# One pool for all eight PSUM banks, a planner that knows the port lock and instruction fetch, and three raw buffers in place of six

## The chip, the cores and the metric

The kernel runs on one core of a Trainium2 chip. The metric is the time of one execution in microseconds (us) of the device; lower is better. Each kernel was run several times beside runs of the kernel before on the same chip. A run is called fast when it lies within 1.5% of the fastest run of the same kernel there, and slow otherwise. Ratios are the mean of one kernel's fast runs over the mean of the other's fast runs of the same rounds, so they are not quite the ratio of the medians that are quoted too. The span of a profile is about 2 us shorter than the time.

## The reference, cut to what matters

```python
# attention half: q, k, v of shape (8, 8, 576, 64)
q_p, k_p = phi(q), phi(k)            # relu, times cos and sin of the position, 128 features
kv  = einsum('bhsf,bhsd->bhfd', k_p, v);  z = sum(k_p, axis=2)
x   = (q_p @ kv) / (q_p @ z + 1e-6)  # (8, 576, 512) once the heads are put together
# mixing half
wq, wk = x @ w_q, x @ w_k            # 512 -> 64
mixed  = (wq @ wk.T / 8) @ x
out    = relu(mixed) @ w_out         # 512 -> 512, the output projection
```

Inputs and output are float32. 29.6 MB are read and 9.4 MB written.

## The kernel before: the parts that matter

The work is cut into 16 steps of the attention half (a step `H` is four heads of one batch entry: 576 KB each of q, k and v), eight batch entries of the mixing half, and 36 row tiles of the output projection (`wo`, four matmuls of 128x512 each). POOL turns the raw inputs into bfloat16 (`rq`, `rk`, `rv`), DVE multiplies k by cos and sin (`mk`, tile `kp`), PE does the rest, ACT and DVE empty PSUM. SP issues all loads and nearly all stores.

The order in which every engine gets its instructions is not written by hand. A planner runs at build time: it keeps a clock for each engine, gives every operation a cost and its data dependences, and always takes the candidate with the smallest start time, less a small bonus for priority. The chip then waits only for data and buffers, but each engine works through its queue in that order.

```python
op(("load", nm, H), {"DMA": 1.51}, [ago(i >= 3, "r" + "qkv"[i % 3], i // 3)])  # i counts from -nraw
...
op(("qT", H), {"PE": .27}, [ago(H, "rq", H), ago(H, "kve", H - 1)], pa, "row")
...
op(("wo", p, rt), {"PE": .86}, need, pw, "full", 1)
...
after = dict(PE=.13, ACT=.07, DVE=.07, POOL=.1, DMA=.4)   # us until a result may be used
...
key = s - .1 * o["prio"]                                  # PE: start, less a tenth of the priority
...
inp = ctx.enter_context(tc.tile_pool(name="inp", bufs=PLAN["nraw"]))   # raw inputs, 6 buffers
...
K0, N0, M0, M1, M2, M3 = 0, 2, 4, 5, 6, 7                 # PSUM banks: qT and kv; numerators; the rest
```

Of the kernel before, what the change touches and what calls it, by code (L numbers as in the profile page):

```python
# [23 lines left out]
PLAN = dict(mk=1.5, pa=7.057, pc=7.377, pm=6.4, pw=5.394, pb=0.0, flex=.249, poe=3.15, pme=3.3,  # L24
            pmk=.82, wo_at=4, nraw=6, nout=10)


def plan_order(NB, par=None):

    par = {**PLAN, **(par or {})}  # L30
    B = NB // 2
    ops = {}

    def op(name, cost, deps, prio=0.0, mode=None, banks=0, frees=None):
        ops[name] = dict(cost=cost, deps=[d for d in dict.fromkeys(deps) if d],
                         prio=prio, mode=mode, banks=banks, frees=frees)
# [5 lines left out]
    for H in range(NB):  # L42
# [11 lines left out]
        op(("qT", H), {"PE": .27}, [ago(H, "rq", H), ago(H, "kve", H - 1)], pa, "row")  # L54
        for r in range(2):
            op(("qe", H, r), {"DVE": .72}, [("qT", H), ago(H > 1, "num", H - 2, r)], 3)
        op(("kv", H), {"PE": .58}, [ago(H, "mk", H), ago(H, "rv", H), ("qe", H, 0),
                                    ("qe", H, 1)], pa, "row")
        op(("kve", H), {"ACT": 1.05, "DVE": .8}, [("kv", H)], 3)
        for r in range(2):  # L60
            prev = ("norm", H, 0) if r else ago(H, "norm", H - 1, 1)
            op(("num", H, r), {"PE": .33}, [("kve", H), ("qe", H, r), prev], pa, "row")
            op(("norm", H, r), {"DVE": 1.08}, [("num", H, r), ago(b > 2, "kx", b - 3)], 2)
# [4 lines left out]
    for b in range(B):  # L68
        old = [("mx", b - 2, j) for j in range(4)] if b > 1 else []
        op(("wqk", b), {"PE": 1.0},  # L70
           [("xe", H, j) for H in (2 * b, 2 * b + 1) for j in range(2)] + [("cw", 0)],
           pc, "full", 2)
        op(("we", b), {"ACT": .66, "DVE": .78}, [("wqk", b)] + old, 4,
# [4 lines left out]
        op(("kx", b), {"PE": .55}, [("wke", b)], pc, "full", 1)  # L78
        op(("kxe", b), {"ACT": .38, "DVE": .44}, [("kx", b)] + old, 4,
# [6 lines left out]
    for p in range(B // 2):  # L86
        for rt in range(9):
# [4 lines left out]
            if p == 0:  # L92
                need += [("cw", c) for c in range(1, 5)]
            op(("wo", p, rt), {"PE": .86}, need, pw, "full", 1)
            i = 9 * p + rt - par["nout"]
            op(("oe", p, rt), {"ACT": .60, "DVE": .71},
               [("wo", p, rt), ago(i >= 0, "st", i // 9, i % 9)], par["poe"],
# [17 lines left out]
    mode, bank, own, done, order, nload = "full", [0.0] * 4, {}, {}, [], 0  # L115
# [6 lines left out]
    while ready:  # L122
        best = None
        for n, t in ready.items():
# [3 lines left out]
            for e, c in o["cost"].items():  # L128
                s, mine = max(free[e], t), None
                if e == "PE":  # L130
                    s = max(free[e] + (.1 if o["mode"] != mode else 0), t)
                    if o["banks"] == 2:
                        u = min((0, 2), key=lambda i: max(bank[i], bank[i + 1]))
                        s, mine = max(s, bank[u], bank[u + 1]), (u, u + 1)
                    elif o["banks"] == 1:
                        s = max(s, min(bank))
                        u = max((i for i in range(4) if bank[i] <= s),
                                key=lambda i: bank[i ^ 1])
                        mine = (u,)
                    key = s - .1 * o["prio"]  # L140
# [11 lines left out]
        if e == "PE":  # L152
            gap = s - free[e]
            if gap > .9 and bank[3] <= free[e]:
                order.append((("warm", int(gap / .45)), "PE", None))
            mode = o["mode"]
        free[e] = s + c
# [23 lines left out]
def kernel(  # L181
# [15 lines left out]
    P = 128  # L197
# [32 lines left out]
    K0, N0, M0, M1, M2, M3 = 0, 2, 4, 5, 6, 7  # L230
# [25 lines left out]
    def warm_up(n):  # L256
        for _ in range(n):
            nc.tensor.matmul(bank(M3)[:, 0, :], warm[:, 0:P], warm,  # L258
                             start=True, stop=True)

    warm_up(13)
# [118 lines left out]
    def qT_mm(H):  # L380
        for c in range(C9):
            for r in range(2):
                nc.tensor.transpose(  # L383
                    bank_h(K0 + r)[:, 0, c * D:(c + 1) * D],
# [3 lines left out]
    def qT_evac(H, r):  # L388
        nc.vector.tensor_mul(  # L389
            qpt_bufs[H % 2][:, r, :, D:SLOTS * D],  # L390
            bank_h(K0 + r)[:, 0:1, 0:HC].to_broadcast([P, 2, HC]), cst)

    def kv_mm(H):
        for c in range(C9):
            for i in range(2):
                for r in range(2):
                    nc.tensor.matmul(  # L397
                        bank(K0 + r)[:, 0, i * (D + 1):(i + 1) * (D + 1)],
# [4 lines left out]
    def kv_evac(H, eng):  # L403
        kv_sb = small.tile([P, 2, KW], BF16, name="kv_sb")
        kv_sh = small.tile([P, 2, D + 1], BF16, name="kv_sh")
        src = bank(K0, 2)
# [5 lines left out]
    def num_mm(H, r):  # L412
# [240 lines left out]
```

## Time and profile before

| what | before |
|---|---|
| time, median of the four runs beside the changed kernel | 133.81 us (133.13 to 136.04) |
| span of the profile | 130.8 us |
| mean clock granted to PE | 0.974 |
| PE busy | 105.8 us |
| data moved | 39.40 MB at 301 GB/s, 375 to 378 while loads last |

POOL's waits for loads in the kernel before (engine, tile and line, what it waited for: us in total, times, longest):

```profile
POOL rq_buf L348 <- DMA raw<-in_q_dram: 7.9, 6, 2.9
POOL v_buf L373 <- DMA raw<-in_v_dram: 6.6, 10, 0.8
POOL rk L348 <- DMA raw<-in_k_dram: 2.7, 5, 1.9
```

POOL stands 17.2 us for loads, spread over the whole loading time.

### The profile page before, as it was taken

Reading aid. Unit: us, or ns where it says so; the run is one execution under the profiler, and the core shown is the slowest. Engines: PE = TensorE matmul, PEld = TensorE weight load, DVE = VectorE, ACT = ScalarE, POOL = GpSimd, SP = SyncE. Lnnn points to the kernel's source line nnn. Section 1 sums busy time; section 2 is a strip of 40 time slices with the busy share of each in tenths; the row PEclk is TensorE's granted clock in tenths of the full one; section 3 lists DMA queues with packets and bytes.
Section 4 is the critical chain, followed back from the end, with each engine's and each line's share of the span. In section 5 each row is a group of like instructions: output and inputs, shape, how many; then the busy total and the mean of one; then the engine's idle time right before and its main releaser. Section 6 shows DMA issues by size and latency. Waiting matters only on the chain.

```text
span 130.8 us, 5363 instructions
## 1 busy us (share of the span) xinstructions
PE 105.8 (81%) x2279; PEld 61.8 (47%) x2279; DVE 93.8 (72%) x153; ACT 78.5 (60%) x154; POOL 76.8 (59%) x121
## 2 busy tenths in 40 slices
PE   5947685885699989986999699889947999899930
PEld 2325253563546546643756366556624664443300
DVE  1065979689994999959999987989659876346200
ACT  6950063658756796639557595787637865655440
POOL 7728988896779999975697876885371000000000
PEclk9999999999959999999999999999999999999995
DMA  3999999999999999999999999999974034837973
GB/s 88 369 383 394 345 310 403 394 388 390 389 393 388 374 391 396 401 378 376 316 393 413 368 359 378 383 373 295 382 214 87 5 80 89 177 75 167 211 226 110
DMA packets 21239, 39.40 MB, mean 301 GB/s; under 512 B 3040, under 2 KB 4576, under 8 KB 21216
## 3 DMA queue, kind: packets, MB, share of 16 engines
q1 hardware_dynamic: 20544, 38.08, 85.0%
q10 hardware_dynamic: 672, 0.98, 2.5%
q8 instruction: 18, 0.29, 0.9%
q14 instruction: 5, 0.04, 0.1%
HBM read 29.62 MB, written 9.44 MB: 299 GB/s over the span
## 4 chain that ended last, share of the span: by engine, by line
PE 43%; DMA 23%; DVE 14%; ACT 5%; POOL 5%; issue 4%; SPq 2%; ACTq 1%; POOLq 0%
PE ps L532 19%; DMA raw<-in_k_dram 12%; DMA raw<-in_q_dram 9%; PE ps L422 5%; PE ps L462 5%; PE ps L397 5%; DVE kp L361 4%; DVE qpt_buf L389 4%; PE ps L492 3%; POOL rk L348 3%; PE ps L447 2%; PE ps L383 2%; DVE x_sb L435 2%; PE ps L508 2%; POOL rq_buf L348 2%
## 5 line engine op out<-in xcount | busy, mean ns | idle before, releaser
L532 PE MATMUL ps<-wo_sb,mix_sb 128*128 128x512 bf16 x144 | 37.3, 386 | 2.0 <-issue 1.7
L348 POOL TENSOR_SCALAR rq_buf<-raw 128x640 bf16<-128x640 f32 (+1 forms) x32 | 26.2, 835 | 9.3 <-DMA raw<-in_q_dram 7.9
L373 POOL TENSOR_SCALAR v_buf<-raw 128x640 bf16<-128x640 f32 (+1 forms) x30 | 27.1, 920 | 7.4 <-DMA raw<-in_v_dram 6.6
L361 DVE TENSOR_TENSOR kp<-rk,cossin 128x2304 bf16<-128x2304 bf16 (+2 forms) x17 | 22.5, 1324 | 11.3 <-ACT rk L346 6.1
L335 ACT COPY o_sb<-ps 128x512 f32<-128x512 f32 x32 | 18.8, 586 | 15.8 <-PE ps L532 12.9
L435 DVE TENSOR_TENSOR x_sb<-ps,rec 128x640 bf16<-128x640 f32 x32 | 26.4, 824 | 1.1
L389 DVE TENSOR_TENSOR qpt_buf<-ps,cst 128x1152 bf16<-128x1152 bf16 x32 | 22.6, 747 | 0.0
L348 POOL TENSOR_SCALAR rk<-raw 128x640 bf16<-128x640 f32 (+1 forms) x30 | 19.5, 669 | 4.2 <-DMA raw<-in_k_dram 2.7
L422 PEld LDWEIGHTS <-qpt_buf 64*128 64x128 bf16 x640 | 14.3, 95 | 14.0 <-issue 13.2
L422 PE MATMUL ps<-kv_sb,qpt_buf 64*128 64x65 bf16 x320 | 16.3, 193 | 4.2 <-DVE x_sb L435 3.7
L532 PEld LDWEIGHTS <-mix_sb 128*128 128x128 bf16 x144 | 11.9, 98 | 15.6 <-issue 4.1
L335 ACT COPY xT_buf<-ps 128x640 bf16<-128x640 bf16 (+1 forms) x25 | 15.7, 650 | 3.0 <-PE ps L447 1.7
L422 PE MATMUL ps<-kv_sh,qpt_buf 64*128 64x65 bf16 x320 | 16.3, 192 | 1.1 <-issue 0.2
L397 PE MATMUL ps<-v_buf,kp 64*128 64x65 bf16 x576 | 13.1, 190 | 3.8 <-DVE qpt_buf L389 2.9
L520 ACT ACTIVATE mix_sb<-ps 128x576 bf16<-128x576 f32 x24 | 14.7, 657 | 2.4 <-PE ps L508 2.4
L397 PEld LDWEIGHTS <-kp 64*128 64x128 bf16 x576 | 10.6, 94 | 8.2 <-issue 3.4
L335 ACT CAST kv_sb<-ps 128x260 bf16<-128x260 f32 x13 | 4.9, 378 | 12.4 <-PE ps L397 12.2
L508 PE MATMUL ps<-wT_buf,kx 64*128 64x288 bf16 x32 | 8.5, 292 | 2.6 <-ACT mix_sb L520 1.9
L258 PE MATMUL ps<-warm 128*128 128x512 bf16 x31 | 9.4, 441 | 1.5 <-DVE warm L254 1.5
L383 PE MATMUL ps<-ident,rq_buf 64*128 64x64 bf16 x288 | 8.1, 192 | 2.6 <-POOL rq_buf L348 1.3
L433 DVE RECIPROCAL rec<-ps 128x10 f32<-128x10 f32 x32 | 6.8, 213 | 4.0 <-PE ps L426 3.8
L462 PE MATMUL ps<-xT_buf,wqk_sb 128*128 128x288 bf16 x64 | 9.2, 287 | 0.0
(51 smaller groups left out, 115.8 us busy)
## 6 DMA issues: line engine op xcount, KB each, us to landing
raw<-in_q_dram SPq DMA_DIRECT2D x15, 576.0 KB, 7.1
raw<-in_k_dram SPq DMA_DIRECT2D x15, 576.0 KB, 7.3
raw<-in_v_dram SPq DMA_DIRECT2D x15, 576.0 KB, 7.2
out_dram<-o_sb SPq DMA_DIRECT2D x67, 128.0 KB, 5.3
wo_f<-in_moe_w_out_dram SPq DMA_DIRECT2D x1, 1024.0 KB, 10.2
out_dram<-o_sb ACTq DMA_DIRECT2D x5, 128.0 KB, 2.9
raw<-in_k_dram ACTq DMA_DIRECT2D x1, 320.0 KB, 4.5
raw<-in_q_dram SPq DMA_DIRECT2D x1, 320.0 KB, 4.2
```

What stands on the lines that cost most here:

```text
L335: nc.scalar.copy(dst, src)
L348: eng.tensor_scalar(dst, src, FMAX, 0.0, op0=ALU.min, op1=ALU.max)
L361: nc.vector.tensor_mul(kp[H][:, 2 * lo:2 * hi], rks[H][:, lo:hi].rearrange("p c i d -> p (c i) d").unsqueeze(2) .to_broadcast([P, 2 * (hi ...
L373: eng.tensor_scalar(dst, src, 1.0, 1.0, op0=ALU.mult, op1=ALU.mult)
L389: nc.vector.tensor_mul(qpt_bufs[H % 2][:, r, :, D:SLOTS * D], bank_h(K0 + r)[:, 0:1, 0:HC].to_broadcast([P, 2, HC]), cst)
L397: nc.tensor.matmul(bank(K0 + r)[:, 0, i * (D + 1):(i + 1) * (D + 1)], kp[H][half_rows(r), 2 * c + i, :, :], v_bufs[H % 3][half_rows(r), c, ...
L422: nc.tensor.matmul(nb[t][:, u, :], qpt_bufs[H % 2][rows, r, w, u * P:(u + 1) * P], mv, start=(u == 0 and w == 0), stop=False)
L435: nc.vector.tensor_tensor(xv[:, h, r], nv[:, :, :, 0:D], rec.to_broadcast([P, 2, SC, D]), op=ALU.mult)
L462: nc.tensor.matmul(bank(m + nh)[:, 0, 0:hs], wqk_sb[:, dmc, :, :], xT_bufs[b % 2][:, dmc, nh * hs:(nh + 1) * hs], start=(dmc == 0), stop=( ...
L508: nc.tensor.matmul(bank(m + r)[:, 0, 0:hs], kxs[b][half_rows(r), i * P:(i + 1) * P], rhs, start=True, stop=True)
L520: nc.scalar.activation(dst, src, AF.Relu, scale=scale_moe)
L532: nc.tensor.matmul(bank(m)[:, 0, :], mixs[bp][:, dmc, rt * P:(rt + 1) * P], wo_sb[:, dmc, :], start=(dmc == 0), stop=(dmc == NDM - 1))
```

## The change

The intent is to let any matmul group use any free PSUM bank, to plan with two effects that the old planner left out (a DVE instruction that shuts POOL out of SBUF, and PE waiting for its next block of instructions), and to choose the planner's values anew, three raw buffers among them.

```diff
-PLAN = dict(mk=1.5, pa=7.057, pc=7.377, pm=6.4, pw=5.394, pb=0.0, flex=.249, ..., wo_at=4, nraw=6, nout=10)
+PLAN = dict(mk=1.4, pa=3.562, pc=4.418, pm=3.974, pw=2.377, pb=0, flex=0.201, ..., wo_at=3, nraw=3, nout=10, ...)
+PE_COUNT = dict(qT=36, kv=72, num=44, xT=36, wqk=16, wk=10, kx=20, mx=4, wo=8)
...
-        op(("qT", H), {"PE": .27}, [ago(H, "rq", H), ago(H, "kve", H - 1)], pa, "row")
+        op(("qT", H), {"PE": .27}, [ago(H, "rq", H), ago(H, "kv", H - 1),
+                                    ago(H > 1, "num", H - 2, 1)], pa, "row", 2)
... (kv, num in the same way: two banks of the pool, freed by the copies that read them)
-    mode, bank, own, done, order, nload = "full", [0.0] * 4, {}, {}, [], 0
+    lock, block, left_in = 0.0, 0.0, 100
+    mode, bank, own, done, order, nload = "full", [0.0] * 8, {}, {}, [], 0
...
+                if n[0] == "mk" or e == "POOL":
+                    s = max(s, lock)
...
+        if n[0] == "mk":
+            lock = s + c
+        elif e == "POOL":
+            lock = max(lock, s + c / 2)
+        elif e == "PE":
+            left_in -= PE_COUNT[n[0]]
+            if left_in < 0:
+                left_in += 256
+                s = max(s, block)
+                block = s + 2.3 + min(3.8, .6 + .8 * max(0.0, free["DMA"] - s))
...
-    K0, N0, M0, M1, M2, M3 = 0, 2, 4, 5, 6, 7
... (every group now gets its bank from the planner)
```

The values that are left out of `PLAN` here are the same as before or are multiplied by zero.

More of the change, by code (lines that the diff above doesn't have):

```diff
@@ L4 @@
 import os
+import random
 from contextlib import ExitStack
@@ L21 @@
 EPS_HI = 9.9837780e-07
-PLAN = dict(mk=1.5, pa=7.057, pc=7.377, pm=6.4, pw=5.394, pb=0.0, flex=.249, poe=3.15, pme=3.3,
-            pmk=.82, wo_at=4, nraw=6, nout=10)
+PLAN = dict(mk=1.4, pa=3.562, pc=4.418, pm=3.974, pw=2.377, pb=0, flex=0.201, poe=6.894,
+            pme=239.564, pmk=16.944, wo_at=3, nraw=3, nout=10, sw=0, amp=0, seed=69325)
+PE_COUNT = dict(qT=36, kv=72, num=44, xT=36, wqk=16, wk=10, kx=20, mx=4, wo=8)
 def plan_order(NB, par=None):
@@ L32, in plan_order @@
     ops = {}
+    rnd = random.Random(par["seed"])
     def op(name, cost, deps, prio=0.0, mode=None, banks=0, frees=None):
         ops[name] = dict(cost=cost, deps=[d for d in dict.fromkeys(deps) if d],
-                         prio=prio, mode=mode, banks=banks, frees=frees)
+                         prio=prio + par["amp"] * rnd.random(),
+                         mode=mode, banks=banks, frees=frees)
     def ago(cond, *name):
@@ L53, in plan_order @@
                par["pmk"])
-        op(("qT", H), {"PE": .27}, [ago(H, "rq", H), ago(H, "kve", H - 1)], pa, "row")
+        op(("qT", H), {"PE": .27}, [ago(H, "rq", H), ago(H, "kv", H - 1),
+                                    ago(H > 1, "num", H - 2, 1)], pa, "row", 2)
         for r in range(2):
-            op(("qe", H, r), {"DVE": .72}, [("qT", H), ago(H > 1, "num", H - 2, r)], 3)
-        op(("kv", H), {"PE": .58}, [ago(H, "mk", H), ago(H, "rv", H), ("qe", H, 0),
-                                    ("qe", H, 1)], pa, "row")
-        op(("kve", H), {"ACT": 1.05, "DVE": .8}, [("kv", H)], 3)
+            op(("qe", H, r), {"DVE": .72}, [("qT", H)], 3,
+               frees=(("qT", H), r))
+        op(("kv", H), {"PE": .58}, [ago(H, "mk", H), ago(H, "rv", H),
+                                    ago(H > 2, "num", H - 3, 1)], pa, "row", 2)
+        op(("kve", H), {"ACT": 1.05, "DVE": .8}, [("kv", H)], 3,
+           frees=(("kv", H), None))
         for r in range(2):
-            prev = ("norm", H, 0) if r else ago(H, "norm", H - 1, 1)
-            op(("num", H, r), {"PE": .33}, [("kve", H), ("qe", H, r), prev], pa, "row")
-            op(("norm", H, r), {"DVE": 1.08}, [("num", H, r), ago(b > 2, "kx", b - 3)], 2)
+            op(("num", H, r), {"PE": .33}, [("kve", H), ("qe", H, r),
+                                        ago(b > 2, "kx", b - 3)], pa, "row", 2)
+            op(("norm", H, r), {"DVE": 1.1}, [("num", H, r)], 2,
+               frees=(("num", H, r), None))
         op(("xT", H), {"PE": .28}, [("norm", H, 0), ("norm", H, 1),
@@ L70, in plan_order @@
         op(("wqk", b), {"PE": 1.0},
-           [("xe", H, j) for H in (2 * b, 2 * b + 1) for j in range(2)] + [("cw", 0)],
+           [("xe", H, j) for H in (2 * b, 2 * b + 1) for j in range(2)] + [("cw", 0)] + old,
            pc, "full", 2)
-        op(("we", b), {"ACT": .66, "DVE": .78}, [("wqk", b)] + old, 4,
+        op(("we", b), {"ACT": .66, "DVE": .78}, [("wqk", b)], 4,
            frees=(("wqk", b), None))
@@ L77, in plan_order @@
         op(("wke", b), {"ACT": .44, "DVE": .34}, [("wk", b)], 4, frees=(("wk", b), None))
-        op(("kx", b), {"PE": .55}, [("wke", b)], pc, "full", 1)
-        op(("kxe", b), {"ACT": .38, "DVE": .44}, [("kx", b)] + old, 4,
+        op(("kx", b), {"PE": .55}, [("wke", b)] + old, pc, "full", 1)
+        op(("kxe", b), {"ACT": .38, "DVE": .44}, [("kx", b)], 4,
            frees=(("kx", b), None))
@@ L93, in plan_order @@
                 need += [("cw", c) for c in range(1, 5)]
+            i = 9 * p + rt - par["nout"]
+            need += [ago(i >= 0, "st", i // 9, i % 9)]
             op(("wo", p, rt), {"PE": .86}, need, pw, "full", 1)
-            i = 9 * p + rt - par["nout"]
             op(("oe", p, rt), {"ACT": .60, "DVE": .71},
-               [("wo", p, rt), ago(i >= 0, "st", i // 9, i % 9)], par["poe"],
+               [("wo", p, rt)], par["poe"],
                frees=(("wo", p, rt), None))
@@ L132, in plan_order @@
                     if o["banks"] == 2:
-                        u = min((0, 2), key=lambda i: max(bank[i], bank[i + 1]))
+                        u = min((0, 2, 4, 6), key=lambda i: max(bank[i], bank[i + 1]))
                         s, mine = max(s, bank[u], bank[u + 1]), (u, u + 1)
@@ L136, in plan_order @@
                         s = max(s, min(bank))
-                        u = max((i for i in range(4) if bank[i] <= s),
+                        u = max((i for i in range(8) if bank[i] <= s),
                                 key=lambda i: bank[i ^ 1])
                         mine = (u,)
-                    key = s - .1 * o["prio"]
+                    key = s - .1 * o["prio"] + (par["sw"] if o["mode"] != mode else 0)
                 elif e == "DMA":
@@ L153, in plan_order @@
             gap = s - free[e]
-            if gap > .9 and bank[3] <= free[e]:
-                order.append((("warm", int(gap / .45)), "PE", None))
+            if gap > .9 and min(bank) <= free[e]:
+                order.append((("warm", int(gap / .45)), "PE", bank.index(min(bank))))
             mode = o["mode"]
+        if n[0] == "mk":
[8 more added lines that the diff above has]
+                block = s + 2.3 + min(3.8, .6 + .8 * max(0.0, free["DMA"] - s))
         free[e] = s + c
@@ L254, with warm_up @@
     nc.vector.memset(warm, 1.0)
-    def warm_up(n):
+    def warm_up(n, m):
         for _ in range(n):
-            nc.tensor.matmul(bank(M3)[:, 0, :], warm[:, 0:P], warm,
+            nc.tensor.matmul(bank(m)[:, 0, :], warm[:, 0:P], warm,
                              start=True, stop=True)
-    warm_up(13)
+    warm_up(13, 7)
     wq_f = consts.tile([P, NDM, DH], FP32)
@@ L378, in half_rows, with qT_mm @@
         return slice(64 * r, 64 * r + 64)
-    def qT_mm(H):
+    def qT_mm(H, m):
         for c in range(C9):
@@ L383, in qT_mm, with qT_evac, kv_mm @@
                 nc.tensor.transpose(
-                    bank_h(K0 + r)[:, 0, c * D:(c + 1) * D],
+                    bank_h(m + r)[:, 0, c * D:(c + 1) * D],
                     rq_bufs[H % 3][half_rows(r), c, :, :],
                     ident[half_rows(r), half_rows(r)])
-    def qT_evac(H, r):
+    def qT_evac(H, r, m):
         nc.vector.tensor_mul(
             qpt_bufs[H % 2][:, r, :, D:SLOTS * D],
-            bank_h(K0 + r)[:, 0:1, 0:HC].to_broadcast([P, 2, HC]), cst)
-    def kv_mm(H):
+            bank_h(m)[:, 0:1, 0:HC].to_broadcast([P, 2, HC]), cst)
+    def kv_mm(H, m):
         for c in range(C9):
@@ L397, in kv_mm @@
                     nc.tensor.matmul(
-                        bank(K0 + r)[:, 0, i * (D + 1):(i + 1) * (D + 1)],
+                        bank(m + r)[:, 0, i * (D + 1):(i + 1) * (D + 1)],
                         kp[H][half_rows(r), 2 * c + i, :, :],
@@ L401, in kv_mm, with kv_evac @@
                         start=(c == 0 and i == 0), stop=(c == C9 - 1 and i == 1))
-    def kv_evac(H, eng):
+    def kv_evac(H, m, eng):
         kv_sb = small.tile([P, 2, KW], BF16, name="kv_sb")
         kv_sh = small.tile([P, 2, D + 1], BF16, name="kv_sh")
-        src = bank(K0, 2)
+        src = bank(m, 2)
         copy(eng, kv_sb, src[:, :, 0:KW])
@@ L410, in kv_evac, with num_mm @@
         kvs[H] = (kv_sb, kv_sh)
-    def num_mm(H, r):
-        nb = [bank(N0 + t)[:, 0, 0:SC * (D + 1)].rearrange(
+    def num_mm(H, r, m):
+        nb = [bank(m + t)[:, 0, 0:SC * (D + 1)].rearrange(
             "p (u e) -> p u e", u=SC) for t in range(2)]
@@ L427, in num_mm, with norm @@
                              eps_t[half_rows(t), :], start=False, stop=True)
-    def norm(H, r):
+    def norm(H, r, m):
         b, h = divmod(H, 2)
-        nv = bank(N0, 2)[:, :, 0:SC * (D + 1)].rearrange("p t (u e) -> p t u e", u=SC)
+        nv = bank(m, 2)[:, :, 0:SC * (D + 1)].rearrange("p t (u e) -> p t u e", u=SC)
         rec = small.tile([P, 2, SC, 1], FP32, name="rec")
@@ L573, in emit @@
         elif kind == "qT":
-            qT_mm(b)
+            qT_mm(b, m)
         elif kind == "qe":
-            qT_evac(b, j)
+            qT_evac(b, j, m)
         elif kind == "kv":
-            kv_mm(b)
+            kv_mm(b, m)
         elif kind == "kve":
-            kv_evac(b, engs[eng])
+            kv_evac(b, m, engs[eng])
         elif kind == "num":
-            num_mm(b, j)
+            num_mm(b, j, m)
         elif kind == "norm":
@@ L585, in emit @@
                 xs[b // 2] = xpool.tile([P, SC, NH, D], BF16, name="x_sb")
-            norm(b, j)
+            norm(b, j, m)
         elif kind == "xT":
@@ L618, in emit @@
         elif kind == "warm":
-            warm_up(b)
+            warm_up(b, m)
     for n, eng, m in plan_order(NB):
-        emit(n, eng, None if m is None else M0 + m)
+        emit(n, eng, m)
 _INS = ['q', 'k', 'v', 'moe_w_q', 'moe_w_k', 'moe_w_out']
```

## The prediction

> **What bounds the kernel now.** I read the busy table and the slices first, then the busy time by stretch, then the matrix engine's waits by stretch, then the chain of waits, then the DMA issues.
>
> The page of the kernel before, its first two parts:
>
> ```profile
> span 130.8 us, 5363 instructions
> ...
> PE 105.8 (81%) x2279; PEld 61.8 (47%) x2279; DVE 93.8 (72%) x153; ACT 78.5 (60%) x154; POOL 76.8 (59%) x121
> ...
> PE   5947685885699989986999699889947999899930
> ...
> DMA  3999999999999999999999999999974034837973
> ```
>
> The reader is to see three stretches. In the first ten or eleven slices (to about 37 us) PE is between a half and nine tenths busy. From there to slice 28 (95 us) PE and the DMA are both near full. After that the loads are over, the DMA has room, and PE alone is near full until 122 us. So no engine is the bound of the whole: 39.40 MB at the 380 to 390 GB/s of the full slices are about 102 us, and PE is busy 105.8 us. The span is 25 us over either because the two do not start together.
>
> Busy time by stretch, and the same for the warm-up matmuls alone (two answers of the windows view):
>
> ```profile
> 8.00:37.00 29.00, 20.50 (x587) 13.51 (x587) 24.40 (x38) 14.10 (x32) 22.28 (x29) 0.97 1.05 378
> 37.00:95.00 58.00, 53.41 (x1279) 32.68 (x1274) 50.03 (x83) 39.52 (x84) 45.91 (x59) 0.99 1.03 375
> 95.00:122.00 27.00, 23.54 (x381) 12.45 (x380) 17.75 (x31) 16.47 (x32) 2.94 (x4) 1.00 0.50 113
> 122.00:131.00 9.00, 3.26 (x15) 1.16 (x12) 0.27 (x1) 2.34 (x4) 0.00 (x0) 0.80 0.65 176
> ...
> 8.00:37.00 29.00, 0.00 (x0) 0.00 (x0) 0.97 1.05 378
> ...
> 8.00:37.00 29.00, 4.89 (x18) 1.22 (x18) 0.97 1.05 378
> ```
>
> The columns are PE, PEld, DVE, ACT, POOL, then clock, DMA share and GB/s. The last two lines are the same stretch for the output projection alone (none at all) and for the warm-up matmuls alone (4.89 us). In 8 to 37 us PE is idle for 29.0 - 20.5 = 8.5 us and does filler for 4.9, so 13.4 us of 29 are not work. In 37 to 95 the idle time is 4.6 us, in 95 to 122 it is 3.5, after 122 it is the tail of copying out and storing. The useful PE work is 15.6 + 53.4 + 23.5 + 3.3 = 95.8 us, or 6.0 us for each of the 16 steps (a step is four heads: 1.77 MB of loads).
>
> PE's waits in 8 to 37 us, then from 37 to 95 us:
>
> ```profile
> PE ps L422 <- DVE x_sb L435: 2.7, 4, 1.1
> PE ps L397 <- DVE qpt_buf L389: 2.2, 6, 0.5
> PE ps L383 <- issue: 1.0, 2, 0.7
> ...
> PE ps L508 <- ACT mix_sb L520: 1.9, 4, 1.1
> ```
>
> The first two are PSUM waits. The second numerator needs the bank pair that the first one's normalisation is still reading, and the k-v product needs the pair that the scaling of qT is still reading, although nothing in their data ties them. The fourth is the same in the pool of the second half: the mixing matmul waits until ACT has emptied a pair.
>
> The chain of waits begins with 5.1, 6.7 and 7.6 us of loads (to 22.5 us), goes through POOL and DVE to 35 us, then is PE almost throughout to 118 us. It touches a load once more:
>
> ```profile
> 85.35 1.29 POOL rq_buf L348 x2
> ...
> 86.99 7.73 DMA raw<-in_k_dram
> ```
>
> That is the last step's k, which lands at 94.75 us. So time won early counts fully only if this load also comes earlier, or if PE has a smaller backlog behind it.
>
> **What the Trainium skill says.** (1) "PSUM — Partial Sum Buffer", its summary of rules, has PSUM guarded bank by bank: read one bank while the matmul writes another. The trace agrees: the waits above are all for a bank that a copy has not left. (2) "SBUF — State Buffer", section "Who interferes with whom": a VectorE instruction with two SBUF inputs blocks a GpSimd instruction that reads SBUF, for the whole instruction. The trace shows the pattern: the product that makes kp (L361, both inputs in SBUF) starts at 29.10 us, and the two POOL casts of v that start at 29.14 take 2.53 us together, where undisturbed ones at 12.94 take 1.31. (3) "Runtime: NRT & Kernel Launch", section "Instruction fetch mechanics": instructions come in blocks of 256 by the sequencer's own DMA queue, which it calls mostly hidden. Here it is not quite hidden: 18 such packets for PE, and PE stands 0.74 us before L383 at 29.9, 0.29 at 36.5 and 1.69 in the middle of an accumulation of L532 at 95.4, with nothing to wait for, each about a microsecond after a block's packet. That is 2.7 us.
>
> **The change, part by part.** No instruction of work is added or taken away: the 64 matmul groups of the attention half (four a step) are only given other banks, so the durations of the rows stay. What moves is the order and the waits.
>
> (a) One pool of four pairs in place of one pair for qT and kv, one for the numerators, two for the rest. Removed: the two waits named in 8 to 37 us, 2.7 + 2.2 = 4.9 us, and with them some of the 4.9 us of filler, which stands in front of the same groups. Not all is won, because that stretch is also held by arrivals: POOL starts q of steps 1 to 6 at 9.93, 14.45, 21.11, 26.51, 33.02 and 38.46 us, 5.7 us apart, and DVE is busy 24.4 of 29. PE work on hand without the output projection is 6.0 - 2.3 = 3.7 us a step (the projection is 36 groups of 0.97 us in 16 steps, 2.2 to 2.3 us). So the gain must be an earlier first projection. It stands at 37.46 us, though step 1's v was cast at 14.25. Adding the durations of the 14 links between gives some 10 us (0.7 + 1.0 + 0.4 + 1.5 + 0.4 + 0.7 + 1.0 + 0.7 + 0.2 + 0.4 + 0.6 + 0.4 + 0.3 + 0.7 = 9.0, and handing over); 23 pass. I take 4 us as won here, of 13.4. The move of the output weights one step earlier (now cast at 31.4 us) goes with it.
>
> (b) In 37 to 95 us the same pool can remove 1.9 us of L508 and 0.8 us of L422. PE is at 92% there and the DMA at 375 GB/s. 1.77 MB of loads and 0.59 MB of stores a step need 6.2 us at 380 GB/s, about PE's 6.0. So I count 1.5 us.
>
> (c) The model of instruction fetch spreads dense small matmuls, and half as many loads queued shortens the fetch: of 2.7 us I count 1.5.
>
> (d) The port model takes off blocked POOL and DVE time. The 30 casts of v cost 27.1 us and the 30 for k 19.5, for equal tiles; with those of q at 26.2 POOL loses about 13 us. Half of that back would be some 0.4 us a step, but POOL still waits 17 us for loads. Directly 0.
>
> (e) Three raw buffers in place of six. Step 1's loads are now issued at 3.39, 4.08 and 4.91 us. With three buffers they wait until step 0's are read: 7.69 (q), 8.28 (k), 9.00 (v). An almost empty queue then serves them: the first 320 KB, among six others, landed 4.2 us after issue, so I estimate 3.5 to 4, and step 1 starts about 1.5 us later than 9.93. Cost 1.5 us at the front. Later one buffer's round is 0.4 (issue) + about 4 (half of the present 7.1 with half queued) + 1.3 to 1.7 on POOL = 5.7 to 6.1 us, against a need of 6.0. No reserve is left, so I add 0.5 us of lateness as a mean of nothing and a few microseconds.
>
> Sum: -4 - 1.5 - 1.5 + 0 + 1.5 + 0.5 = -5.0 us. The half-clock spell of 3.4 us in the slice at 33.5 us (0.83 in 30 to 40 us) costs about 1.7 us at present and may go if PE is denser there; a third of it, 0.5, is counted. So 133.5 - 5.5 = 128.0.
>
> **The rivals.** First: the loads become the bound. For it speaks the full DMA up to 95 us and the round of 6 us in (e). Each us in which the DMA has nothing to do early is a us by which the last load lands later, and stores that come sooner delay it too. If k of the last step lands 4 us later, at 99, and the 36 us behind it shrink only to 33, the kernel takes about 134: the same. Against it speaks that POOL consumes steps 6.0 us apart anyway, held by PE, so that a sixth buffer mostly queues.
>
> Second: DVE is the bound of the front (24.4 of 29 us, and 9.4 of 10 in 60 to 80). Then freed banks only move PE's wait to DVE's queue and the win in (a) is 1 to 2 us: about 131. Third, the good one: the backlog of PE goes. At 95 us 17 of 36 output row tiles are still to do. If the projection starts by 30 us and PE stays full, the 7 us before 37 are nearly all won and the fetches too: 122 to 124. The order is found by a search over a model of these same costs, which favours this over the first.
>
> **Range and chances.** 128.0, and 122.5 to 132.5 for 8 in 10: the lower end is the third rival whole, the upper the second with a late load. The 2% line is 130.8; the sum would have to fail by more than half. Faster 0.77, same 0.19, slower 0.04.
>
> **What would show it right or wrong.** Right: L422 waits for x_sb and L397 for qpt_buf near zero; the first L532 well before 37 us; filler below 18; POOL's first q of step 1 near 11.5 us; the DMA below 390 GB/s before 37 us; loads landing in about 4 us; last k at or before 95 us. Wrong: POOL waiting for loads much above 17 us and PE for rq_buf or kp in the middle (first rival), or DVE above 90% to 60 us with PE waiting for it under other names (second).

## The result, and the profile after

The changed kernel takes 159.6 us (median of four runs, 157.1 to 161.62) against 133.81: the ratio of the fast runs is 1.182, with a 95% interval of 1.164 to 1.201. It is 26 us slower (24 by the fast runs, 157.9 against 133.6), far outside the range of 122.5 to 132.5.

The page of the changed kernel, its first two parts:

```profile
span 156.7 us, 5383 instructions
...
PE 114.1 (73%) x2278; PEld 70.9 (45%) x2278; DVE 93.8 (60%) x155; ACT 78.1 (50%) x152; POOL 71.1 (45%) x121
...
PE   6766483986986079966089993849896898999820
...
PEclk9999968589999758999857999555799599999995
DMA  4978899995889989999698899988993033489885
```

The span grew by 25.9 us. PE is busy 8.3 us longer for the same work (114.1 in place of 105.8), as its granted clock is 0.855 on average in place of 0.974, and it stands still 17.6 us longer (156.7 - 114.1 = 42.6 us against 130.8 - 105.8 = 25.0). DVE's busy time is the same, POOL's is 5.7 us lower. The digits of the clock drop to 5 in or just after slices in which PE stands. The Trainium skill, "TensorE: Matmul & The Clock Gate", section "HAM oscillation — how this bites in real kernels", gives the rule of leaving no gaps in PE's work longer than about 3.4 us. The trace agrees in part: a gap of 5.0 us from about 50.4 to 55.4 us goes with a clock of 0.66 from 50 to 60 us. But so long a gap is not needed: in the changed kernel a spell at half clock begins at about 121.5 us, where the longest wait since 110 us was 0.6 us, and in the kernel before one begins at 35.3 us, where the longest since 24 us was 0.7 us.

Busy time by stretch in the changed kernel (PE, PEld, DVE, ACT, POOL, clock, DMA share, GB/s):

```profile
8.00:37.00 29.00, 19.60 (x472) 12.79 (x465) 20.07 (x35) 9.83 (x22) 15.27 (x22) 0.82 0.88 291
37.00:95.00 58.00, 43.12 (x1011) 28.23 (x1012) 39.86 (x65) 31.79 (x66) 33.53 (x47) 0.88 0.90 293
95.00:120.00 25.00, 18.34 (x438) 13.05 (x437) 17.88 (x27) 11.66 (x27) 16.64 (x22) 0.73 0.86 285
120.00:147.00 27.00, 25.31 (x329) 14.02 (x329) 14.67 (x29) 16.64 (x31) 0.00 (x0) 0.94 0.54 117
```

The last column is the news. The data rate is 285 to 293 GB/s where it was 375 to 378, and POOL still works on loads after 95 us, where the kernel before was all but done (2.94 us of POOL work left there against 16.64 here). The chain of waits of the changed kernel (start, us, what) says the same:

```profile
48.29 5.77 DMA raw<-in_v_dram
54.21 1.32 POOL v_buf L397 x2
55.54 4.76 DMA raw<-in_v_dram
60.45 1.64 POOL v_buf L397 x2
62.11 5.55 DMA raw<-in_v_dram
67.81 1.38 POOL v_buf L397 x2
```

A load, the POOL instructions that free its buffer, the next load into that buffer: one turn takes 6 to 9 us and carries on to 102 us without a break. POOL's waits for loads are now

```profile
POOL rq_buf L372 <- DMA raw<-in_q_dram: 16.2, 10, 4.4
POOL rk L372 <- DMA raw<-in_k_dram: 13.6, 11, 3.3
POOL v_buf L397 <- DMA raw<-in_v_dram: 13.5, 12, 2.6
```

43.3 us in place of 17.2. And the DMA issues (KB each, us from issue to landing), q of the kernel before first, then the three of the changed kernel:

```profile
raw<-in_q_dram SPq DMA_DIRECT2D x15, 576.0 KB, 7.1
...
raw<-in_q_dram SPq DMA_DIRECT2D x15, 576.0 KB, 5.4
raw<-in_k_dram SPq DMA_DIRECT2D x15, 576.0 KB, 5.6
raw<-in_v_dram SPq DMA_DIRECT2D x15, 576.0 KB, 5.4
```

A load lands after 5.4 to 5.6 us with three of them allowed at once; with six in the kernel before it was 7.1 to 7.3. Half as many requests did not make the landing half as long. POOL's first q casts of the steps after the first lie 7.2 us apart on average from 12.1 us to 113.4, where they lay 6.0 apart from 9.9 to 93.4.

How one late load stops PE for 5 us is seen in the timeline of the changed kernel:

```profile
50.19 0.19 PE L450 MATMUL ps<-eps_t,ones_t 64*128 64x5 bf16 x2
...
51.65 1.29 POOL L372 TENSOR_SCALAR rk<-raw 128x640 bf16<-128x640 f32 x2 [3.31 <-DMA raw<-in_k_dram]
...
52.98 1.36 DVE L385 TENSOR_TENSOR kp<-rk,cossin 128x2304 bf16<-128x2304 bf16 x1 [4.31 <-POOL rk L372]
...
54.26 0.21 DVE L457 RECIPROCAL rec<-ps 128x10 f32<-128x10 f32 x1
54.50 0.83 DVE L459 TENSOR_TENSOR x_sb<-ps,rec 128x640 bf16<-128x640 f32 x1
...
55.38 0.66 PE L407 MATMUL ps<-ident,rq_buf 64*128 64x64 bf16 x18 [5.01 <-DVE x_sb L459]
```

Read it backwards. PE's next group waits for the normalisation (`x_sb`). The numerators for that were there by 50.4 us, but in DVE's queue the product `kp` stands in front, and that waits for POOL, which waits for the load of k. The line of L450 is the last of four such groups since 49.2 us, each in two banks, and DVE empties none of the four before 54.26 us: all eight banks are full, so PE has no bank for its next group. The profile names DVE; what holds it up is a load.

### The profile page after: what moved, and what is told of

Same layout as the page of the kernel before. It is cut to its first block, busy times and chain, and to the rows that moved or that the text cites. A ratio compares the mean times of both kernels' runs of the same rounds, so it can differ in the third digit from the quotient of the medians.

```text
span 156.7 us, 5383 instructions
## 1 busy us (share of the span) xinstructions
PE 114.1 (73%) x2278; PEld 70.9 (45%) x2278; DVE 93.8 (60%) x155; ACT 78.1 (50%) x152; POOL 71.1 (45%) x121
## 4 chain that ended last, share of the span: by engine, by line
DMA 50%; PE 21%; POOL 12%; issue 4%; ACT 4%; DVE 2%; SPq 2%; ACTq 2%; POOLq 0%; DVEq 0%
DMA raw<-in_v_dram 32%; DMA raw<-in_q_dram 15%; PE ps L556 11%; POOL v_buf L397 7%; DMA raw<-in_k_dram 4%; POOL rq_buf L372 3%; PE ps L446 2%; ACT o_sb L359 2%; PE ps L486 2%; ACTq L566 2%; SPq L272 1%; PE ps L532 1%; PE ps L516 1%; PE ps L471 1%; PE ps L421 1%
## 5 line engine op out<-in xcount | busy, mean ns | idle before, releaser
L556 PE MATMUL ps<-wo_sb,mix_sb 128*128 128x512 bf16 x144 | 36.0, 386 | 3.7 <-DVE qpt_buf L413 2.2
L372 POOL TENSOR_SCALAR rq_buf<-raw 128x640 bf16<-128x640 f32 (+1 forms) x32 | 20.9, 670 | 18.1 <-DMA raw<-in_q_dram 16.2
L372 POOL TENSOR_SCALAR rk<-raw 128x640 bf16<-128x640 f32 (+1 forms) x30 | 19.4, 666 | 15.8 <-DMA raw<-in_k_dram 13.6
L407 PE MATMUL ps<-ident,rq_buf 64*128 64x64 bf16 x288 | 9.8, 210 | 16.4 <-DVE x_sb L459 9.7
L421 PE MATMUL ps<-v_buf,kp 64*128 64x65 bf16 x576 | 15.2, 206 | 6.7 <-POOL v_buf L397 4.0
L421 PEld LDWEIGHTS <-kp 64*128 64x128 bf16 x576 | 12.9, 104 | 10.6 <-issue 5.2
L446 PEld LDWEIGHTS <-qpt_buf 64*128 64x128 bf16 x640 | 15.2, 106 | 3.6 <-issue 3.1
L407 PEld LDWEIGHTS <-rq_buf 64*128 64x128 bf16 x288 | 7.5, 107 | 18.3 <-issue 9.9
L282 PE MATMUL ps<-warm 128*128 128x512 bf16 x30 | 10.4, 496 | 1.5 <-DVE warm L278 1.5
L486 PE MATMUL ps<-xT_buf,wqk_sb 128*128 128x288 bf16 x64 | 11.1, 325 | 0.0
L471 PE MATMUL ps<-ident,x_sb 64*128 64x64 bf16 x288 | 9.4, 214 | 0.9 <-DVE x_sb L459 0.9
## 6 DMA issues: line engine op xcount, KB each, us to landing
out_dram<-o_sb SPq DMA_DIRECT2D x67, 128.0 KB, 3.7
out_dram<-o_sb ACTq DMA_DIRECT2D x5, 128.0 KB, 3.1
```

The costliest lines, as they stand in the source:

```text
L372: eng.tensor_scalar(dst, src, FMAX, 0.0, op0=ALU.min, op1=ALU.max)
L407: nc.tensor.transpose(bank_h(m + r)[:, 0, c * D:(c + 1) * D], rq_bufs[H % 3][half_rows(r), c, :, :], ident[half_rows(r), half_rows(r)])
L421: nc.tensor.matmul(bank(m + r)[:, 0, i * (D + 1):(i + 1) * (D + 1)], kp[H][half_rows(r), 2 * c + i, :, :], v_bufs[H % 3][half_rows(r), c, ...
L446: nc.tensor.matmul(nb[t][:, u, :], qpt_bufs[H % 2][rows, r, w, u * P:(u + 1) * P], mv, start=(u == 0 and w == 0), stop=False)
L486: nc.tensor.matmul(bank(m + nh)[:, 0, 0:hs], wqk_sb[:, dmc, :, :], xT_bufs[b % 2][:, dmc, nh * hs:(nh + 1) * hs], start=(dmc == 0), stop=( ...
L556: nc.tensor.matmul(bank(m)[:, 0, :], mixs[bp][:, dmc, rt * P:(rt + 1) * P], wo_sb[:, dmc, :], start=(dmc == 0), stop=(dmc == NDM - 1))
```

## The experiments

All keep the results correct except the two that leave out stores. Medians are of all runs; where fast runs differ from the median, both are given.

### First: are the three raw buffers the cause?

```diff
 o_after_b6, o_after_b4 (changed kernel; the planner still plans for three)
-    inp = ctx.enter_context(tc.tile_pool(name="inp", bufs=PLAN["nraw"]))
+    inp = ctx.enter_context(tc.tile_pool(name="inp", bufs=6))      # 4 in o_after_b4
 o_before_b3 (kernel before; the planner still plans for six)
+    inp = ctx.enter_context(tc.tile_pool(name="inp", bufs=3))
 after_n6 (changed kernel, planner and pool alike)
-    ... nraw=3 ...
+    ... nraw=6 ...
```

> The changed kernel's order of instructions exactly, with six raw buffers behind it in place of three. Theory A (three raw buffers bound the loads by their round trip): about 132, between 126 and 138; POOL's q casts 6.0 to 6.2 us apart in place of 7.0, DMA near 375 GB/s to the end of the loads, clock above 0.95. Theory B (the order itself, planned by a model that takes a load for 1.51 us, with the freed banks, is the loss): over 146, clock still near 0.86.

Measured: 145.96 us (141.57 to 147.88; the one fast run is the 141.57). Between the two theories.

> The kernel before's order exactly (it was planned for six), with three raw buffers. Theory A: about 155, between 148 and 165, POOL's q casts 7 us apart, DMA near 300 GB/s. Theory B: between 134 and 141.

Measured: 156.51 us, ratio 1.171 (1.161 to 1.180). As theory A had it. Its loads land in 5.4 to 5.6 us and its data rate from 37 to 95 us is 301 GB/s.

> The changed kernel with six raw buffers for the planner too, so that it plans another order. Theory A: as with six buffers behind the old order, or a few us better, 125 to 134, since the order then suits the buffers. Theory B: over 145, since the model of banks, port and fetch is still there.

Measured: 144.21 us, ratio 1.084 (1.078 to 1.091). Against theory A.

> The changed kernel's order with four raw buffers. Theory A: one buffer more takes a quarter off the time that a round of 7.0 us costs for three loads (7.0 x 3/4 = 5.3 us a step, below PE's 6.0), so most of the loss is gone: 132 to 142. Theory B: 150 or more.

Measured: 148.9 us, ratio 1.115 (1.104 to 1.126). One buffer more takes 11 of the 14 us that three more take (9.4 of 16.4 by fast runs), but the range of neither theory held.

With the order of the changed kernel, going from six buffers to three costs 13.6 us by the medians (159.6 - 146.0) and 16.4 by the fast runs (157.9 - 141.6, of which the second is a single run). With the order of the kernel before it costs 23 by either. So the buffers are one large cause. But with six buffers the changed kernel still loses 8 to 11 us of 133 by fast runs. In after_n6 POOL hardly waits for loads: 5.3 us for q, 0.6 for v and 0.5 for k. (In o_after_b6, whose order is still the one planned for three, POOL waits 29.0 us for them, so there the loads stay part of the account.) A second cause is in the order.

### Second: which part of the planner makes the order worse?

Each of these has six raw buffers.

```diff
 banks_only:   changed kernel, old PLAN values, both models off
 models_only:  kernel before + the lock and the fetch lines of the diff above
 params_only:  kernel before + the new PLAN values (nraw=6)
 banks_params: changed kernel, new values (nraw=6), both models off
 (models off)
-                if n[0] == "mk" or e == "POOL":
-                    s = max(s, lock)
...
-            if left_in < 0:
+            if False and left_in < 0:
```

> Six raw buffers, the old planner values, no port or fetch model; only the pool of eight banks (with the waits that go with it) is new. Theory C (the old split of the banks held the attention half back and so kept the projection in step; freed, attention runs ahead, DVE fills and the projection piles up at the end): 141 or more, and a run of ten or more projection groups at the end of PE's work. Theory D (the port and fetch models spoil the order): 128 to 134. Theory E (any new order of this greedy planner loses, since only the old one was picked on the chip): 135 to 142.

Measured: 147.69 us, ratio 1.100 (1.089 to 1.111).

> The kernel before with only the port lock and the instruction fetch added to its planner. Theory C: 132 to 136. Theory D: 141 or more. Theory E: 135 to 142.

Measured: 140.35 us, ratio 1.057 (1.049 to 1.064).

> The kernel before with only the new planner values (priorities, flex, the weights' place), six raw buffers kept. Theories C and D: 131 to 136. Theory E: 135 to 142.

Measured: 137.48 us; its one fast run is 134.44.

> The changed kernel with six raw buffers and both models off: banks and values new. Theory C: as banks_only, 141 or more. Theory D: 128 to 135. Theory E: 135 to 145, not tied to banks_only.

Measured: 134.53 us; its one fast run is 131.55. The kernel before took 133.35 in the same rounds.

No theory holds for all four. The freed banks cost 14 us with the old values, and with the new ones they gain 3 (134.53 against 137.48). The models cost 7 us with the old banks, and 10 us with the new (144.2 against 134.5; 13 by fast runs, with one fast run of banks_params). I looked for something that any of the parts can bring about and that the slow ones share. The number of the projection's weight loads that PE has done by 95 us is such a thing. It is in part an effect, since a kernel that is slow for any reason has done less by then, so it points to a cause and does not show one. These are the first 95 us of the projection alone (PE, PEld, clock, DMA share, GB/s), of the kernel before, then of after_n6:

```profile
0.00:95.00 95.00, 22.03 (x85) 7.15 (x86) 0.98 1.02 366
```

```profile
0.00:95.00 95.00, 13.25 (x40) 3.79 (x40) 0.91 0.95 339
```

86 of 144 against 40. The others with six buffers are 80 (params_only), 76 (banks_params), 52 (banks_only) and 48 (models_only): the three with 76 or more take 133 to 138 us, the three with 52 or fewer 140 to 148. In after_n6 the attention half runs ahead, DVE fills (53.82 us busy of the 58 from 37 to 95 us, 50.03 in the kernel before), PE stands for DVE, and the projection is left to a stretch in which no other engine has much to do. The full DVE is not common to the slow ones: banks_only has 50.52. In after_n6 the DMA ran at 108 GB/s from 95 to 122 us, and then the last stores had to go out at 205.

### Third: is it the place of the projection? Undone in one direction, made in the other

```diff
 after_n6_brake: after_n6, one more condition for the planner alone
+        w = int(2.25 * (H - 4)) - 1
         op(("qT", H), {"PE": .27}, [ago(H, "rq", H), ago(H, "kv", H - 1),
-                                    ago(H > 1, "num", H - 2, 1)], pa, "row", 2)
+                                    ago(H > 1, "num", H - 2, 1),
+                                    ago(w >= 0, "wo", w // 9, w % 9)], pa, "row", 2)
 before_pw0: kernel before
-    ... pw=5.394 ...
+    ... pw=0 ...
 after_lat: changed kernel, three buffers
-    after = dict(PE=.13, ACT=.07, DVE=.07, POOL=.1, DMA=.4)
+    after = dict(PE=.13, ACT=.07, DVE=.07, POOL=.1, DMA=3.9)
 after_n6_lockonly: after_n6
-            if left_in < 0:
+            if False and left_in < 0:
```

> after_n6 (pool, both models, six raw buffers; 144.2) with one more condition for its planner alone: the queries of step H go to PE only after 2.25 x (H - 4) tiles of the output projection have. Nothing else that the chip waits for is added. Theory F (what cost 10 us with six buffers is that the order lets the attention half run ahead and leaves the projection to the end): 132 to 137, about 80 of the 144 projection matmuls before 95 us in place of 40. Theory G (the pool's order is worse for another reason, such as PE blocked behind single late operands): 141 or more.

Measured: 134.63 us (133.79 to 135.42, all fast), the kernel before beside it 135.14 (one fast run, 131.74).

> The kernel before with one number changed, the priority of the projection in its planner from 5.394 to 0, half a microsecond of preference; the projection then comes late in its order (on average after 14.3 steps' numerators, not 11.4). Theory F: 141 to 150, 50 or fewer projection matmuls before 95 us. Theory G: 132 to 137.

Measured: 150.03 us; its fast runs are 149.6 and 147.99.

The projection's first 95 us in after_n6_brake, then in before_pw0:

```profile
0.00:95.00 95.00, 18.56 (x62) 6.30 (x76) 0.96 1.01 364
```

```profile
0.00:95.00 95.00, 9.21 (x28) 3.25 (x36) 0.91 0.95 339
```

The weight loads are the better count, since some matmul records are missing from these traces. A change of the order alone, which makes the chip wait for no new data, takes 10 us off one kernel and adds 15 to the other (17 by fast runs), and each time the number of early projection loads moves as expected. The planner plans the whole order anew in each, so other operations move too; what the two edits share is the place of the projection. In the timeline of before_pw0 the deferred work can be seen whole, 61 matmuls in one run at the end:

```profile
121.92 14.67 PE L532 MATMUL ps<-wo_sb,mix_sb 128*128 128x512 bf16 x61 [0.22 <-issue]
```

This is what the Trainium skill, "Perfetto Trace Analysis", section "Optimization Strategy", says of kernels with several regimes: performance may be gained by interleaving the regimes. Here it is the difference between 134.6 and 144.2 us.

> The changed kernel with three raw buffers kept, but its planner told that a load lands 3.9 us after its 1.51, not 0.4, as the changed kernel's trace shows (5.4). Theory A with F: the order improves (the projection comes early), but the round of a buffer stays, q casts 7 us apart, last v after 112 us: 146 to 154. Theory H (the planner's wrong landing time was the whole of it): under 138.

Measured: 153.88 us; its one fast run is 149.55. The projection came early again (72 of its weight loads by 95 us), POOL's q casts stayed 7.8 us apart, and the last v was cast at 128 us. So a planner that knows the landing time better does not make three buffers good. Theory H is out.

> after_n6 with the instruction fetch taken out of its planner, the port lock kept. The projection comes after 11.6 steps on average, as in the kernel before. Theory F: 131 to 136, which puts the 10 us on the fetch model. Theory G: 139 or more.

Measured: 134.46 us (133.1 to 136.37). Of the two models, the one of instruction fetch is what put the projection late in after_n6; with the lock alone 72 of the 144 weight loads are done by 95 us.

### Fourth: where did the gain of the freed banks go?

```diff
 before_half, brake_half (kernel before, after_n6_brake): store one half of each tile, wrong on purpose
-        for hi in range(2):
+        for hi in range(1):
 pool_brake: banks_params with the condition of after_n6_brake
 brake_n8: after_n6_brake with nraw=8
```

> The kernel before with only one of the two halves of each output tile stored (wrong result on purpose): 4.7 MB less on the DMA, nothing else. Theory I (before, PE sets the pace in the middle, so the DMA is not the bound there): 130 to 133, of which up to 1 us is the shorter last store. Theory J says the same.

Measured: 129.62 us (fast runs 128.98 to 129.88), beside 133.47 (fast runs 130.7 and 131.09).

> after_n6_brake with half of the stores left out in the same way. Theory I (with the banks freed the loads set the pace, and stores delay them): 4 us or more below after_n6_brake, 126 to 130. Theory J: 131 to 134, as much as in before_half.

Measured: 130.68 us (130.47 to 131.25, all fast).

Both lose about 4 us of their median, 3.9 and 4.0 (134.63 to 130.68, from two chips). By fast runs it is 1.5 us in the kernel before (130.9 to 129.4) and 3.8 in the other (134.6 to 130.8). So stores cost time in both; the medians say that they cost the two kernels the same, against theory I, the fast runs lean towards it. The two runs do not settle it. The edit also takes 36 of the 72 store issues off the queues, so it does not isolate the bytes.

> Pool of eight banks, new values, six raw buffers, the condition of after_n6_brake, no port or fetch model. Theory J: 126 to 131, below the kernel before. Theory I: 132 to 136, no different from after_n6_brake.

Measured: 131.24 us (129.56 to 131.91), the kernel before beside it 133.47 (130.7 to 137.63). The fast runs are the same: 130.8 on average for five of pool_brake's six, 130.9 for the two of eleven of the kernel before that count as fast. So it is a tie in like states. Its median is 2.2 us lower because it was seldom slow; whether that is its doing, these few runs do not say.

> after_n6_brake with eight raw buffers. Theory I: the DMA is already full, so within 1.5 us of after_n6_brake's 134.6, 133 to 136. If instead loads are asked for too late with six: 129 to 132.

Measured: 137.28 us (all fast). Neither range held. It was also planned anew, for eight, and its order has 80 early weight loads, so the place of the projection is not the reason. What is stays open. One candidate, not tested: PE's waits called issue are 4.8 us there and 2.8 in after_n6_brake.

### Fifth: why do three buffers cost so much?

```diff
 after_split, before_split: the changed kernel; the kernel before with three buffers
-    inp = ctx.enter_context(tc.tile_pool(name="inp", bufs=3))
+    inp = ctx.enter_context(tc.tile_pool(name="inp", bufs=6))
...
+                raw[nm, H, lo] = inp.tile([P, 2, 5 * D], FP32, name="raw")   # one for each half
```

> The changed kernel's order, with each of the three raw buffers split into two that are loaded and freed separately (twice the load issues, half the size). Theory K (the round of a buffer sets the pace): a half lands sooner and is freed after one POOL instruction, not two, so a step takes near 6 us, not 7: 146 to 152, near the 146 of six whole buffers. Theory L (the bytes in flight set it): 156 or more.

Measured: 155.02 us; its fast runs are 152.46 and 154.5.

> The same with the kernel before's order, which with three whole buffers took 156.5. Theory K: 136 to 148. Theory L: 153 or more.

Measured: 154.38 us; its fast runs are 152.59 and 150.59.

Each gains about 4 us in fast runs over its whole-buffer form (153.5 against 157.9, 151.6 against 156.0), far less than theory K had, and not nothing as theory L had for the first. A step still takes 7.2 us in after_split. The DMA issues of after_split say why K fell:

```profile
raw<-in_q_dram SPq DMA_DIRECT2D x16, 320.0 KB, 5.1
...
raw<-in_q_dram SPq DMA_DIRECT2D x16, 256.0 KB, 5.1
```

Half the size lands after 5.1 us, the whole after 5.4. I had taken a half to land much sooner. Six halves allow as many bytes at once as three wholes, and both the landing time and the data rate stayed: from 8 to 37 us the changed kernel has 291 GB/s and after_split 302. The same order with four whole buffers has 322 there and with six 360 (o_after_b4, o_after_b6). So six requests of half the size do not do what six of the whole size do; what helps is more bytes asked for at once, which is what buffers four to six provide.

### The runs with correct results in one table

| kernel | raw buffers | early projection weight loads, of 144 | fast runs, mean (count) | median of all |
|---|---|---|---|---|
| before | 6 | 86 | 130.9 to 133.6, by session | 133.35 to 135.14, by session |
| pool_brake | 6 | 84 | 130.8 (5) | 131.24 |
| params_only | 6 | 80 | 134.4 (1) | 137.48 |
| banks_params | 6 | 76 | 131.6 (1) | 134.53 |
| after_n6_brake | 6 | 76 | 134.6 (4) | 134.63 |
| after_n6_lockonly | 6 | 72 | 134.0 (3) | 134.46 |
| o_after_b6 | 6 | 57 | 141.6 (1) | 145.96 |
| banks_only | 6 | 52 | 146.5 (3) | 147.69 |
| models_only | 6 | 48 | 140.5 (4) | 140.35 |
| after_n6 | 6 | 40 | 144.5 (4) | 144.21 |
| before_pw0 | 6 | 36 | 148.8 (2) | 150.03 |
| brake_n8 | 8 | 80 | 137.2 (4) | 137.28 |
| o_after_b4 | 4 | 57 | 148.5 (3) | 148.9 |
| changed kernel | 3 | 56 | 157.9 (2) | 159.6 |
| o_before_b3 | 3 | 60 | 156.0 (3) | 156.51 |
| after_lat | 3 | 72 | 149.6 (1) | 153.88 |
| after_split | 6 halves | 56 | 153.5 (2) | 155.02 |
| before_split | 6 halves | 67 | 151.6 (2) | 154.38 |

With six buffers a count of 72 or more goes with 131 to 138 us and one of 57 or fewer with 140 to 150. Within the slow group the count does not rank them, so it is not a formula.

## Why the prediction was wrong

The predicted time was 128.0 us, the measured one 159.6. By the steps of the prediction:

**(e), three raw buffers: mis-sized, and the first cause.** It gave 1.5 us at the front and 0.5 later, from a landing time of "about 4 (half of the present 7.1 with half queued)". The start was right: step 1 began at 12.1 us, where 11.5 was expected. The round was not. The landing took 5.4 us, so one turn of a buffer takes about 0.4 + 5.4 + 1.3 = 7.1 us and more, where PE needs a step every 6.0. The text had said that no reserve was left, and then priced the lack of a reserve at 0.5 us. Measured, the term is 13.6 us with the changed order and 23 with the order before (medians; 16.4 and 23 by fast runs). Fifteen steps of loads at 1.2 us more each (7.2 against 6.0) are 18 us, an estimate that lies between the two.

**"What moves is the order and the waits": the second cause, and a step that was missing.** The sum counted waits that the new order removes and none that it adds. It even gave credit: "The order is found by a search over a model of these same costs, which favours this over the first". The order with six buffers is 10 to 12 us worse (144.2 and 146.0; 8 to 11 by fast runs), and a condition that only holds the attention half back brings it to 134.6. A planner's order is as good as its model. This one lets a block of PE instructions begin no sooner than 2.9 to 6.1 us after the block before it, the more the further behind the DMA is, while all the fetch waits of the kernel before that the trace shows are 2.7 us in 18 blocks; and it lets a load be used 0.4 us after its 1.51 us of transfer. The planner can be run by itself from the kernel files. With the changed values its own clock ends at 125.1 us with three buffers and at 131.1 with six; without the fetch lines at 121.0 and 120.0; with the landing time of after_lat at 140.2 and 127.8. So the fetch lines made three buffers look 6 us better, and a truer landing time would have made them look 12 us worse. On the chip three took 157.9 and six 144.5. That taking the fetch model out restores the order was run (after_n6_lockonly, 134.46).

**(a) and (b), the freed banks: the mechanism was right, the 5.5 us were not there.** In the first 37 us of after_n6_brake the two PSUM waits are gone from the list of PE's waits. These are the largest that are left:

```profile
PE ps L473 <- DVE x_sb L461: 2.0, 2, 1.0
PE ps L423 <- DVE kp L387: 1.4, 2, 0.9
PE ps L423 <- POOL v_buf L399: 1.3, 1, 1.3
PE ps L409 <- POOL rq_buf L374: 1.2, 3, 0.6
```

Each is a wait for data: the normalised x that the transpose reads, the products of k, the casts of v and q. PE's busy time from 8 to 37 us is 19.96 us, where it was 20.50; without the filler it is 16.1 where it was 15.6. The first projection, expected 4 us before 37.5 us, starts at 35.4 us there and at 32.6 in pool_brake. The waits took other names, as the second rival said, though that rival expected 131 us. Why the whole then stays at the kernel before's time and not 1 to 2 us below is not settled: theory I, that the loads are now the pace, has the fast runs for it and the medians against it.

**(c), fetch, and (d), the port lock: the numbers came, but by luck.** PE's waits called issue fell from 3.1 us before to 0.2 us in the changed kernel, where 1.5 us had been counted; POOL's busy time fell from 76.8 to 71.1 us and its casts of q from 835 to 670 ns. But the kernel before with three buffers, planned without either model, shows the same: no wait called issue in its list, 70.8 us and 672 ns. So these came with the buffers. With six buffers the lock and fetch models leave POOL at 76.2 us (models_only). The fetch model does cut PE's waits called issue with the new banks and values, from 8.3 us (after_n6_lockonly) to 1.7 (after_n6), and the kernel is 10 us slower for it.

**The half-clock spell: wrong.** A third of it was counted as a gain. It lies at 35.3 to 38.7 us, not in a slice at 33.5. PE stood more, not less, and its clock fell from 0.974 to 0.855. How much of the 26 us the lower clock costs by itself, no run isolates; the 8.3 us more of PE's busy time are an upper bound for the matmuls alone.

**A misread count.** The prediction has 17 of 36 output row tiles left at 95 us. The trace shows 86 of 144 weight loads done by then, so 14.5 tiles are left. No term of the sum rests on it.

**The rivals.** The first one, loads as the bound, is what happened with three buffers, though by the turn of a buffer and not by a full DMA (293 GB/s from 37 to 95 us), with the sign that its text gave (POOL waiting far above 17 us: 43.3). It had been given 134 us at worst, from a last k at 99 us. The last q was cast at 113.4. The chance of 0.04 for slower was the largest mistake of judgement: the text had found the round of 5.7 to 6.1 us against a need of 6.0, and one more microsecond of landing was well within the error of that estimate.

## What to carry to other kernels

Count a buffer's whole turn (issue, landing, the read that frees it) against the time that a step may take, with a landing time that is measured under traffic and not scaled by queue depth; if the two are about equal, expect a loss that is paid at every step. When an order comes from a planner, check its prices against the trace before trusting its optimum, and look at where the deferrable work went: here 40 early projection loads in place of 76 went with a loss of 10 us (after_n6 against after_n6_brake, one planner condition apart). Freeing a resource that held one half of a kernel back can let that half run ahead; put the brake back on purpose, in the order.

## What the Trainium skill lacked or had wrong

- "DMA: Bandwidth & Descriptors" has a fit for one DMA on the GpSimd path (section "Anatomy of one DMA — SWDGE (gpsimd) path", about 2 us plus the bytes at 436 GB/s: 3.4 us for 576 KB, an estimate from that page). For loads issued from SP under traffic, the runs show 5.4 to 5.6 us with three of 576 KB allowed at once, 5.8 to 6.2 with four, 7.1 to 7.3 with six in the kernel before, and 5.1 us for halves of 256 and of 320 KB of q. None of the pages that I read tells how many bytes must be under way to keep the DMA full; here three loads gave 267 to 301 GB/s from 8 to 95 us in the two kernels, and six 375 to 378 in the kernel before.
- "Runtime: NRT & Kernel Launch", section "Instruction fetch mechanics", calls the cost of a block mostly hidden. The kernel before shows 2.7 us in three places, the longest 1.69 us; after_n6_lockonly shows 8.3 us of waits called issue, the two longest (2.6 and 1.9 us) within a microsecond of a block's packet, and still planning against them cost 10 us (144.2 against 134.5).
- "Perfetto Trace Analysis" advises interleaving of regimes; it gives no way of measuring it. Counting the deferrable instructions done by a fixed time was enough here (76 against 40).
